# Windowed attention and two feed-forward layers on one core: weight tiles of two row halves, a 16-bit sign operation, and a new program order

## The chip, the cores and the metric

The kernel runs on one core of a Trainium2 chip. A core has TensorE (PE, the matrix engine; its weight loads are listed apart as PEld), VectorE (DVE), ScalarE (ACT), GpSimd (POOL) and SyncE (SP), which here only issues DMAs. The metric is the device time of one execution in microseconds, the median of the runs.

## The reference, cut to what matters

Attention with a window of 32 positions to each side plus 32 global positions, then a layer that takes the maximum of three products, then a gated layer. Batch 4, 8 heads, 512 local and 32 global positions, head size 64; 2,176 tokens of 512 features go through the two layers.

```python
s_ll = np.where(mask, scale * q_l @ k_l.T, -1e9)            # |i - j| <= 32
a_l = softmax(concat([scale * q_l @ k_g.T, s_ll]))
out_l = a_l @ concat([v_g, v_l])
out_g = softmax(scale * q_g @ concat([k_g, k_l]).T) @ concat([v_g, v_l])
x = concat([out_g, out_l])                                  # 2176 x 512
h = np.maximum(np.maximum(x @ w1, x @ w2), x @ w3)          # 512 -> 768
x = h @ w_out                                               # 768 -> 512
gate = 1.0 / (1.0 + np.exp(-(x @ w_gate)))                  # 512 -> 1536
out = (gate * (x @ w_val)) @ moe2_w_out                     # 1536 -> 512
```

The weights of both layers come as 64-bit floats, the rest as 32-bit floats.

## The kernel before

Attention is done in 32 units: a batch, a half of its positions, and a pair of heads. Four units make a chunk of 256 tokens (288 with the global ones, in every second chunk), so there are eight chunks. Of a unit, PE transposes queries and keys (units 0 to 7, line 532; later ones are transposed by DVE), makes the scores (619), global scores for pairs of units (645, 647), transposes the probabilities (683; later ones go through a DMA transpose) and makes the value products (770, later 780 and 785). In between DVE adds the mask and finds the maxima (625), ACT takes exponentials (661), DVE divides (675). The global rows of a batch have transposes (738) and value products (813, 849) of their own.

The first layer (`moe1_l1`) makes, for a chunk, a block of 128 of the 768 columns (six blocks, `f`) and each of the three matrices (`wi`), one product over four blocks of 128 rows; ACT or DVE folds it into the maximum (890, 893, 896). Chunk 0 uses the weights as plain 32-bit floats (882). The other chunks use a high part and a low part of weights and tokens, three matmuls for one (`mm3`, lines 321 to 323). The second layer (`moe1_l2`, line 918 for chunk 0) follows chunk by chunk. The gated layer (1038) and its output (1225) come last, as seven products for eight by a Strassen scheme.

Each weight tile of the first two layers is fetched and converted by `conv_a(i)`: 18 tiles of w1, w2 and w3 (`i = 3 f + wi`) and 6 of w_out, each 128 partitions by 512 pairs of words. A tile of w1 holds 128 columns and all four row blocks. `to_f32` turns a 64-bit float into a 32-bit one: ACT cuts the low word to three bits (285) and scales the high word (289), DVE puts the sign into the low word (291) and joins the two (294). Then ACT rounds the high part (312) and POOL subtracts it for the low part (271). The same `to_f32` serves the gated layer's weights (`w_prep`, 12 tiles of 1,024 elements) and its output weights (`wo_pre`, 6 of 1,024).

Every step of every unit, product and tile is an entry of a list; `ORDER`, a table of 3,388 numbers, says in which order the entries are issued, and by that the order of instructions on every engine and of the DMAs on SP's queue. An engine takes its instructions in that order, whatever they wait for.

Of the kernel before, what the change touches and what calls it, by code (L numbers as in the profile page):

```python
# [12 lines left out]
U32 = mybir.dt.uint32  # L13
AF = mybir.ActivationFunctionType
ALU = mybir.AluOpType
AX = mybir.AxisListType

P = 128
# [185 lines left out]
def kernel(  # L204
# [17 lines left out]
    nc = tc.nc  # L222
# [58 lines left out]
    def to_f32(raw, low_on_act, out=None):  # L281
# [4 lines left out]
        else:  # L286
            nc.vector.tensor_scalar(out=lo, in0=lo.bitcast(U32), scalar1=2.0 ** -29, scalar2=7.0, op0=ALU.mult, op1=ALU.min)
        yield
        nc.scalar.mul(f32(hi), f32(hi), 2.0 ** -112)
        yield  # L290
        nc.vector.scalar_tensor_tensor(out=lo, in0=hi, scalar=-2147483648, in1=lo,
                                       op0=ALU.bitwise_and, op1=ALU.bitwise_or)
        yield
        nc.vector.scalar_tensor_tensor(out=hi if out is None else out, in0=hi, scalar=3, in1=lo,
# [462 lines left out]
    xt = {}  # L757
# [719 lines left out]
```

## Time and profile before

| | |
|---|---|
| median of three runs | 809.6 us (809.15, 809.6, 814.51) |
| the profiled execution | 812.87 us, span 811.0 us |
| mean granted clock of PE | 0.996 |
| PE busy | 788.9 us, 97% |
| DVE busy | 599.6 us, 74% |
| ACT busy | 472.7 us, 58% |
| POOL busy | 148.8 us, 18% |

The span runs from the first to the last instruction; the time has 1.87 us more around it. A busy PE counts matmuls in flight, which overlap; where they come without a gap, PE sets the time of that stretch.

### The profile page before, as it was taken

The page shows a single profiled execution, that of the slowest core. Times are in us where ns is not written, and L with a number is a line of the kernel's source. Part 1 is how long each engine was busy: PE and PEld are TensorE (multiplying, and loading weights), DVE is VectorE, ACT ScalarE, POOL GpSimd, SP SyncE. Part 2 cuts the span into 40 slices and gives each one's busy share as a digit, 9 for nine tenths or more (in the row PEclk, how much of TensorE's full clock was granted, in tenths as well). Part 3 has the DMA queues.
Part 4 walks back from the last instruction along what each step waited for, and adds up shares of the span by engine and source line. Part 5 has one row for each costly group of instructions (what it writes and reads, how often), then busy time and mean ns, then how long its engine had stood idle before and what let it go on. Part 6 is the DMA issues. An engine that isn't in the chain of part 4 may idle for free.

```text
span 811.0 us, 18055 instructions
## 1 busy us (share of the span) xinstructions
PE 788.9 (97%) x6854; PEld 751.8 (93%) x6854; DVE 599.6 (74%) x1291; ACT 472.7 (58%) x1131; POOL 148.8 (18%) x149
## 2 busy tenths in 40 slices
PE   5999998999999999999999999999999999999998
PEld 3687798998999999899999999999999999999998
DVE  4799895876767676874876888788675858967773
ACT  6897775756446664563647656665636366444442
POOL 3241565243332413332120000000000000000000
PEclk9899999999999999999999999999999999999999
DMA  8998254545556553453425355956422469555411
GB/s 202 265 248 212 60 101 87 102 93 104 107 101 109 96 113 66 101 117 75 181 90 191 101 158 175 317 175 231 147 101 91 163 207 311 166 162 164 142 34 58
DMA packets 217590, 116.07 MB, mean 143 GB/s; under 512 B 161056, under 2 KB 204576, under 8 KB 217504
## 3 DMA queue, kind: packets, MB, share of 16 engines
q1 hardware_dynamic: 216960, 114.80, 52.2%
q8 instruction: 53, 0.87, 0.5%
q14 instruction: 33, 0.27, 0.1%
q10 hardware_dynamic: 544, 0.13, 0.1%
HBM read 74.91 MB, written 28.57 MB: 128 GB/s over the span
## 4 chain that ended last, share of the span: by engine, by line
PE 73%; SPq 8%; issue 6%; DMA 5%; DVE 3%; POOL 2%; ACT 2%; DVEq 0%; POOLq 0%; ACTq 0%
PE pa L1038 18%; PE pe L1038 9%; PE pa L1225 9%; PE ps L321 7%; PE ps L323 7%; PE ps L322 6%; PE pb L1038 4%; PE pe L1225 4%; PE pb L1225 2%; SPq L514 2%; SPq L513 2%; PE sp L619 2%; DMA vr<-in_v_g_dram 1%; PE ps L918 1%; POOL m L271 1%
## 5 line engine op out<-in xcount | busy, mean ns | idle before, releaser
L1038 PE MATMUL pa<-m,m 128*128 128x384 f32 (+1 forms) x864 | 154.1, 327 | 0.0
L321 PE MATMUL ps<-xt,m 128*128 128x288 f32 (+1 forms) x504 | 147.4, 292 | 3.5 <-DVE h L896 2.2
L323 PE MATMUL ps<-xt,m 128*128 128x288 f32 (+1 forms) x504 | 146.6, 291 | 0.0
L322 PE MATMUL ps<-xt,m 128*128 128x288 f32 (+1 forms) x504 | 145.3, 288 | 1.1 <-DVE xt L798 0.9
L1038 PEld LDWEIGHTS pa<-m,m 128*128 128x128 f32 x864 | 144.3, 188 | 0.2
L321 PEld LDWEIGHTS ps<-xt,m 128*128 128x128 f32 x504 | 94.8, 188 | 7.8 <-issue 2.7
L322 PEld LDWEIGHTS ps<-xt,m 128*128 128x128 f32 x504 | 94.7, 188 | 1.5 <-DVE xt L798 1.1
L323 PEld LDWEIGHTS ps<-xt,m 128*128 128x128 f32 x504 | 94.7, 188 | 0.0
L1044 ACT COPY sn<-pa 128x384 f32<-128x384 f32 (+1 forms) x108 | 49.0, 462 | 73.0 <-PE pa L1038 72.6
L1038 PE MATMUL pe<-m,m 128*128 128x384 f32 (+1 forms) x432 | 80.2, 327 | 0.0
L1038 PEld LDWEIGHTS pe<-m,m 128*128 128x128 f32 x432 | 72.5, 188 | 0.1
L1225 PE MATMUL pa<-m,m 128*128 128x256 f32 x576 | 71.9, 283 | 0.0
L1225 PEld LDWEIGHTS pa<-m,m 128*128 128x128 f32 x576 | 70.4, 192 | 0.1
L661 ACT ACTIVATE sm<-sm,st 128x224 f32<-128x224 f32 x128 | 60.8, 481 | 13.3 <-DVE st L625 13.0
L896 DVE TENSOR_TENSOR h<-ps,h 128x288 f32<-128x288 f32 (+1 forms) x90 | 38.9, 436 | 34.9 <-PE ps L323 23.5
L271 POOL TENSOR_TENSOR h<-h,h 128x288 fp32r<-128x288 f32 (+1 forms) x42 | 39.4, 942 | 103.1 <-ACT h L901 102.6
L707 DVE TENSOR_TENSOR pc<-sm,pc 64x512 f16<-64x512 f32 (+1 forms) x72 | 52.0, 723 | 8.1 <-ACT pc L704 6.9
L625 DVE CUSTOM_DVE_ANT_0 sm<-sp,mask 128x224 f32<-128x224 f32 x128 | 44.9, 381 | 7.9 <-PE sp L619 7.4
L321 PE MATMUL ps<-h,m 128*128 128x288 f32 (+1 forms) x168 | 49.4, 294 | 0.0
L1163 ACT CAST m<-m 128x768 fp32r<-128x768 f32 x44 | 35.8, 835 | 23.0 <-DVE m L1174 7.5
L704 ACT CAST pc<-sm 64x512 f16<-64x512 f32 (+1 forms) x72 | 39.3, 545 | 16.7 <-DVE sm L675 15.1
L323 PE MATMUL ps<-h,m 128*128 128x288 f32 (+1 forms) x168 | 48.9, 291 | 0.0
(193 smaller groups left out, 1628.7 us busy)
## 6 DMA issues: line engine op xcount, KB each, us to landing
m<-in_moe_w_dram SPq DMA_DIRECT2D x18, 512.0 KB, 5.5
gd<-sgt SPq DMA_DIRECT2D x48, 192.0 KB, 2.8
m<-gd SPq DMA_DIRECT2D x6, 1536.0 KB, 7.3
m<-in_moe_w_val_dram SPq DMA_DIRECT2D x6, 1024.0 KB, 5.3
wr<-in_moe_w_out_dram SPq DMA_DIRECT2D x6, 1024.0 KB, 6.0
m<-in_moe_w_gate_dram SPq DMA_DIRECT2D x5, 1024.0 KB, 7.6
vr<-in_v_l_dram SPq DMA_DIRECT2D x48, 96.0 KB, 2.5
x2d<-x2s SPq DMA_DIRECT2D x32, 128.0 KB, 2.0
```

Of the source, the lines that this page charges most:

```text
L271: nc.gpsimd.tensor_tensor(out=out, in0=a, in1=f32(b), op=ALU.subtract)
L321: nc.tensor.matmul(ps, lhsT=wh, rhs=xh, start=first, stop=False)
L322: nc.tensor.matmul(ps, lhsT=wh, rhs=xl, start=False, stop=False)
L323: nc.tensor.matmul(ps, lhsT=wl, rhs=xh, start=False, stop=last)
L625: nc.vector.tensor_tensor_reduce(out=sm[:, hh, j], in0=sp[hh][:, j, 0:224], in1=mask[:, half + j, :], scale=-SC, scalar=3.0e38, op0=ALU.ad ...
L661: nc.scalar.activation(sm4[:, i], sm4[:, i], AF.Exp, bias=st[:, 0, i:i + 1], scale=-1.0, accum_out=st[:, 2, i:i + 1])
L704: nc.scalar.copy(d, s_)
L707: nc.vector.tensor_tensor(out=l_, in0=s_, in1=h_, op=ALU.subtract)
L896: nc.vector.tensor_tensor(out=a, in0=ps[:, 0:n], in1=a, op=ALU.max)
L1038: nc.tensor.matmul(ps, lhsT=w[l][:, a, i], rhs=x[m][:, i], start=(k in (1, 2, 5) and i + l + m == 0), stop=(k in (2, 3, 4) and i == 1 and ...
L1044: nc.scalar.copy(t[:, 0:n], pend[u]["a"][:, 0:n])
L1225: nc.tensor.matmul(ps, lhsT=g[l][:, f], rhs=wo_op(b, f, m), start=(k in (1, 2, 5) and f + l + m == 0), stop=(k in (2, 3, 4) and f == 5 and ...
```

## The change

Three things. A tile of w1, w2 or w3 now holds 256 columns and two of the four row blocks (tile `f` of a pair `fp`: row half `kh`), so a product reads two tiles, and the runs in memory are twice as long. The sign word is made by an operation with one input: it takes the top 16 bits of the high word, keeps bit 15, and writes the top 16 bits of the low word, which are zero otherwise. And `ORDER` is another permutation of the same 3,388 entries.

```diff
+U16 = mybir.dt.uint16
...
 ORDER = [
-    153, 154, 57, 87, 0, 256, 56, 62, 63, 64, 67, 68, 69, 74, 58, 70, 71, 59, 1854, 161, 162, 95, 96, 75, 76, 77, 78,
...
-        nc.vector.scalar_tensor_tensor(out=lo, in0=hi, scalar=-2147483648, in1=lo,
-                                       op0=ALU.bitwise_and, op1=ALU.bitwise_or)
+        half = raw.bitcast(U16)
+        nc.vector.tensor_scalar(out=half[:, :, 1], in0=half[:, :, 3], scalar1=0x8000, scalar2=None, op0=ALU.bitwise_and)
...
     def conv_a(i):
         f, wi = divmod(i, 3) if i < 3 * NF1 else (i - 3 * NF1, 3)
+        fp, kh = divmod(f, 2)
...
-            nc.sync.dma_start(out=raw.rearrange("p (k f) t -> p k (f t)", k=KD),
-                              in_=src[:, f * 2 * P:(f + 1) * 2 * P].rearrange("(k p) f -> p k f", p=P))
+            nc.sync.dma_start(out=raw.rearrange("p (k f) t -> p k (f t)", k=2),
+                              in_=src[kh * 2 * P:(kh + 1) * 2 * P, fp * 4 * P:(fp + 1) * 4 * P].rearrange("(k p) f -> p k f", p=P))
...
     def moe1_l1(c, f, wi, hold):
+        cols = slice(P * (f % 2), P * (f % 2) + P)
+        tiles = [(wi, f - f % 2 + k // 2) for k in range(KD)]
...
-                nc.tensor.matmul(ps[:, 0:n], lhsT=ww[wi, f][:, k], rhs=xt[c, k][:, 0, 0:n], start=(k == 0), stop=(k == KD - 1))
+                nc.tensor.matmul(ps[:, 0:n], lhsT=ww[tiles[k]][:, k % 2, cols], rhs=xt[c, k][:, 0, 0:n], start=(k == 0), stop=(k == KD - 1))
...
-            wt = wa[wi, f]
+            wt = wa[tiles[k]]
...
-            mm3(ps[:, 0:n], (wt[:, 0, k], wt[:, 1, k]), (x[:, 0, 0:n], x[:, 1, 0:n]), k == 0, k == KD - 1)
+            mm3(ps[:, 0:n], (wt[:, 0, k % 2, cols], wt[:, 1, k % 2, cols]), (x[:, 0, 0:n], x[:, 1, 0:n]), k == 0, k == KD - 1)
```

Three places show the new order. In its rows the line numbers after the change are two to four higher; `tq` and `tk` are transposes of queries and keys, `sp` scores, `sg` global scores, `tp` transposes of probabilities, `ot` value products, `ps` with `xw` products of the first layer, and `m` with a number is a tile that was loaded (the numbers differ between the two kernels).

PE, the transposes of the second chunk's first unit (`m_289` before, `m_236` after) and what stands around them; before:

```order
L683 MATMUL tp<-ident,sm 128x128 x8
L619 MATMUL sp<-kw,qw 128x224 x4
L532 MATMUL tq<-ident,m_88 128x128 x2
L532 MATMUL tk<-ident,m_137 128x128 x2
L532 MATMUL tk<-ident,m_138 128x64
L532 MATMUL tq<-ident,m_289 128x128 x2
L532 MATMUL tk<-ident,m_258 128x128 x2
L532 MATMUL tk<-ident,m_259 128x64
L645 MATMUL sg<-kw,qgz_82 64x256 x2
L647 MATMUL sg<-kw,qgz_82 64x32 x2
```

and after:

```order
L685 MATMUL tp<-ident,sm 128x128 x8
L621 MATMUL sp<-kw,qw 128x224 x4
L647 MATMUL sg<-kw,qgz_82 64x256 x2
L649 MATMUL sg<-kw,qgz_82 64x32 x2
L534 MATMUL tq<-ident,m_236 128x128 x2
L534 MATMUL tk<-ident,m_287 128x128 x2
L534 MATMUL tk<-ident,m_288 128x64
```

The global scores of the first pair moved ahead of these transposes; those of the third unit, behind the scores before, stand further up.

PE, chunk 0 in the first layer, from the sixth unit's transposes on; before:

```order
L683 MATMUL tp<-ident,sm 128x128 x8
L619 MATMUL sp<-kw,qw 128x224 x4
L882 MATMUL ps_722<-xw,m_457 128x256 x4
L882 MATMUL ps_729<-xw,m_399 128x256 x4
L770 MATMUL ot<-pw,m_488 64x128 x16
L882 MATMUL ps_794<-xw,m_395 128x256 x4
L882 MATMUL ps_799<-xw,m_397 128x256 x4
L882 MATMUL ps_813<-xw,m_502 128x256 x4
L882 MATMUL ps_832<-xw,m_344 128x256 x4
L738 MATMUL tpg<-ident,eg 128x128 x5
L882 MATMUL ps_854<-xw,m_380 128x256 x4
L683 MATMUL tp<-ident,sm 128x128 x4
```

and after, from the score block on:

```order
L621 MATMUL sp<-kw,qw 128x224 x4
L772 MATMUL ot<-pw,m_581 64x128 x8
L886 MATMUL ps_741<-xw,m_577 128x256 x2
L886 MATMUL ps_741<-xw,m_544 128x256 x2
L886 MATMUL ps_755<-xw,m_529 128x256 x2
L886 MATMUL ps_755<-xw,m_594 128x256 x2
L886 MATMUL ps_761<-xw,m_529 128x256 x2
L886 MATMUL ps_761<-xw,m_594 128x256 x2
L740 MATMUL tpg<-ident,eg 128x128 x5
L886 MATMUL ps_780<-xw,m_639 128x256 x2
L886 MATMUL ps_780<-xw,m_574 128x256 x2
L772 MATMUL ot<-pw,m_581 64x128 x8
```

Each product has two tiles now; one unit's value products moved ahead of the first of this group, and the global transposes moved up.

DVE, the conversions behind the first six tiles; before, up to the tile of that group's second product (`m_399`):

```order
L291 SCALAR_TENSOR_TENSOR m_399<-m_399 128x512
L294 SCALAR_TENSOR_TENSOR m_395<-m_395 128x512
L294 SCALAR_TENSOR_TENSOR m_399<-m_399 128x512
L688 COPY pw<-tp 128x512
L625 ISA sm,st<-sp,mask 128x224
```

and after, up to the second tile of that group's first product (`m_544`):

```order
L293 TENSOR_SCALAR m_574<-m_574 128x512
L293 TENSOR_SCALAR m_577<-m_577 128x512
L295 SCALAR_TENSOR_TENSOR m_574<-m_574 128x512
L295 SCALAR_TENSOR_TENSOR m_577<-m_577 128x512
L293 TENSOR_SCALAR m_594<-m_594 128x512
L733 RECIPROCAL stg<-stg 128x1
L295 SCALAR_TENSOR_TENSOR m_594<-m_594 128x512
L293 TENSOR_SCALAR m_544<-m_544 128x512
L295 SCALAR_TENSOR_TENSOR m_544<-m_544 128x512
```

The tile that the second product of the group needed was the tenth to be joined; the first product of the new group needs the eleventh.

## Rows read from the trace of the kernel before

**Rows 1.** The page's first part: busy us (share of the span) and instructions.

```profile
PE 788.9 (97%) x6854; PEld 751.8 (93%) x6854; DVE 599.6 (74%) x1291; ACT 472.7 (58%) x1131; POOL 148.8 (18%) x149
```

**Rows 2.** Stages: length, busy PE, PEld, DVE, ACT, POOL, PE clock, DMA share, GB/s.

```profile
0.00:20.00 20.00, 11.66 (x53) 7.51 (x53) 9.51 (x37) 12.43 (x42) 6.39 (x26) 1.00 0.85 203
20.00:40.00 20.00, 17.98 (x149) 13.45 (x148) 15.33 (x39) 16.36 (x52) 4.39 (x3) 0.83 0.93 265
40.00:60.00 20.00, 19.77 (x130) 16.10 (x130) 19.02 (x47) 19.28 (x51) 8.87 (x6) 1.00 0.95 246
60.00:100.00 40.00, 37.56 (x243) 31.57 (x242) 37.54 (x90) 30.65 (x81) 14.26 (x11) 1.00 0.56 139
100.00:400.00 300.00, 294.23 (x3515) 277.42 (x3514) 212.18 (x604) 174.33 (x517) 107.93 (x98) 1.00 0.51 101
400.00:811.00 411.00, 407.68 (x2772) 405.77 (x2771) 306.07 (x478) 219.64 (x393) 6.94 (x6) 1.00 0.49 160
```

**Rows 3.** PE's waits: for whom, us in total, times, longest.

```profile
PE tq L532 <- DMA m<-in_q_l_dram: 8.1, 4, 3.6
PE ps L321 <- DVE h L896: 2.2, 1, 2.2
...
PE og L849 <- DMA ptg<-pcg: 1.2, 1, 1.2
...
PE ps L322 <- DVE xt L798: 0.9, 1, 0.9
...
PE ot L770 <- DVE pw L688: 0.7, 1, 0.7
```

**Rows 4.** PE's timeline, 19 to 24 us: start, length, instructions, idle time before.

```profile
19.73 0.30 PE L532 MATMUL tq<-ident,m 128*128 128x128 f32 x1 [3.61 <-DMA m<-in_q_l_dram]
20.95 0.48 PE L532 MATMUL tq<-ident,m 128*128 128x128 f32 x1 [0.92 <-DMA m<-in_q_l_dram]
...
22.08 1.12 PE L645 MATMUL sg<-kw,qgz 128*64 128x256 f32 x4
22.98 0.37 PE L647 MATMUL sg<-kw,qgz 128*64 128x32 f32 x4
```

**Rows 5.** Columns of rows 2, from 20.5 to 27.2 us.

```profile
20.50:27.20 6.70, 6.25 (x29) 4.42 (x30) 4.04 (x9) 3.75 (x13) 1.29 (x1) 0.50 0.86 252
```

**Rows 6.** DMA issues by line: count, KB each, median us to landing.

```profile
m<-in_moe_w_dram SPq DMA_DIRECT2D x18, 512.0 KB, 5.5
...
m<-in_moe_w_out_dram SPq DMA_DIRECT2D x6, 512.0 KB, 4.7
```

**Rows 7.** DVE's groups by form: count, busy us, mean ns of one, idle before.

```profile
L291 DVE SCALAR_TENSOR_TENSOR m<-m 128x512 int32<-128x512 int32 x24 | 19.5, 819 | 1.7 <-ACT m L289 1.6
...
L595 DVE CAST vb<-vr 128x512 bf16<-128x512 f32 x24 | 10.5, 440 | 16.4 <-POOL vr L593 13.1 <-DMA qr<-in_q_l_dram 3.1
...
L733 DVE TENSOR_SCALAR eg<-eg,stg 128x640 f32<-128x640 f32 x8 | 5.9, 734 | 0.2
```

**Rows 8.** DVE's timeline, three places between 53 and 91 us.

```profile
53.21 1.29 DVE L294 SCALAR_TENSOR_TENSOR m<-m 128x512 int32<-128x512 int32 x2
...
56.35 1.68 DVE L294 SCALAR_TENSOR_TENSOR m<-m 128x512 int32<-128x512 int32 x1
...
89.94 0.69 DVE L294 SCALAR_TENSOR_TENSOR m<-m 128x512 int32<-128x512 int32 x1
```

**Rows 9.** POOL's timeline from 54 us.

```profile
54.38 3.10 POOL L271 TENSOR_TENSOR m<-m,m 128x512 fp32r<-128x512 f32 x2 [6.96 <-ACT m L312]
```

**Rows 10.** PE's timeline, four places between 53 and 92 us.

```profile
53.23 3.73 PE L882 MATMUL ps<-xw,m 128*128 128x256 f32 x16
56.89 1.98 PE L770 MATMUL ot<-pw,m 96*64 96x128 f32 x32
...
69.58 0.66 PE L683 MATMUL tp<-ident,sm 128*128 128x128 f32 x4 [1.16 <-DVE pwg L744]
...
90.73 1.54 PE L918 MATMUL ps<-hw,m 128*128 128x256 f32 x6 [1.28 <-ACT vb L591]
```

More of the change, by code (lines that the diff above doesn't have):

```diff
@@ L308, in conv_a @@
         hi = f32(raw[:, :, 1])
-        ww[wi, f] = hi.rearrange("p (k f) -> p k f", k=KD) if cols else hi
+        ww[wi, f] = hi.rearrange("p (k f) -> p k f", k=2) if cols else hi
         yield
@@ L314, in conv_a @@
         sub(t[:, 1], hi, t[:, 0])
-        wa[wi, f] = t.rearrange("p l (k f) -> p l k f", k=KD) if cols else t
+        wa[wi, f] = t.rearrange("p l (k f) -> p l k f", k=2) if cols else t
         yield
```

337 rows, old and new, of the table ORDER are left out of this document.

## The prediction

> **What bounds the kernel now.** I read the engines' totals first, then the table by stage, then who makes TensorE (PE) wait, then the timeline at those places. PE is busy for 788.9 us of the 811.0 us span [rows 1], so all that any edit can return is the 22 us in which it is not, and what it does slowly. By stage [rows 2] PE lacks 8.3 us in the first 20 us, 2.0 in the next 20, 0.2 from 40 to 60, 2.4 from 60 to 100, 5.8 in the 300 us from 100 to 400, and 3.3 after 400, nearly all of which is the tail behind the last matmul. The last stage holds everything that the gated layer does; no reordering there can win. The reader is to see two more things in the same table. From 40 to 100 us VectorE (DVE) works 56.6 of 60 us and ScalarE (ACT) 49.9, so while PE looks full, DVE is as full, and it is DVE that hands PE its weights. And from 20 to 40 us the granted clock is 0.83: it is 0.50, the lower level of 1.2 GHz, from 20.5 to 27.2 us [rows 5], right after PE stood idle for 3.6 and 0.9 us.
>
> The waits of PE are few: 8.1 us in all for query rows, 3.6 of it in one piece, then single ones of 2.2, 1.2, 0.9 and 0.7 us [rows 3] and two of 1.2 and 1.3 in the stretch where DVE is full [rows 10]. The long one is in rows 4: the transposes of the second chunk's first unit begin at 19.73 us, when their query rows have landed, after 3.61 us of idle time; the second half begins at 20.95, and everything behind them on PE waits.
>
> **The change, part by part.** The sum is made against the profiled execution, 812.87 us (span 811.0 plus 1.87 around it), which lies 3.3 us above the median of the three runs, 809.6; differences carry over.
>
> *Loads.* Eighteen weight loads stay 512 KB each, but their runs in memory go from 1 KB to 2 KB, and the packets are halved. The nearest row is the six loads of the output matrix, also 512 KB, whose runs are 4 KB: 4.7 us to landing against 5.5 [rows 6]. So each load gains between 0 and 0.8 us. The DMA engines are 0.85 to 0.95 busy for the first 60 us [rows 2], so shorter traffic is real there, but only where PE waits for a load. That is the one place of rows 4: three weight loads are queued on SP ahead of the second chunk's rows, before and after alike, and the bytes ahead are the same. Three times 0.8 would be 2.4, but they overlap in flight and PE waits for the rows behind them; I take 0.4 (from 0 to 2.4).
>
> *Sign word.* 42 operations with two inputs become operations with one. 18 of them (1,024 elements) lie behind 400 us, where PE waits for nothing: 0. The 24 of 512 elements took 0.819 us each [rows 7], 0.69 when alone, and an operation of the same kind beside a GpSimd subtraction took 1.68 [rows 8, 9]. The new form is not in the trace. Bounds: the one-input cast of 512 elements took 0.440 us, and the one-input operation with a scalar on 640 took 0.734 [rows 7], which scaled to 512 at its own 1.15 ns an element is 0.59. I take the middle, 0.52, since the instruction is that of the second row and the width nearer that of the first: 0.30 saved, 24 times, 7.2 us of DVE work (5.5 to 9.1), all of it between 12 and 93 us, where DVE is the fuller engine.
>
> The Trainium skill ("VectorE: DVE Perf Modes", section "Mode 2×_2P — use both read ports for one tensor") says that an operation with one source in SBUF handles two elements a cycle, fp32 included; by it I estimate 512 / 2 / 0.96 GHz plus the row's overhead, 0.34 us. The 734 ns row with one source [rows 7] does not agree, as it ran near one element a cycle. By the rule the saving would be 11.5 us of DVE work instead of 7.2, and the forecast below about 1 us lower. "SBUF — State Buffer", section "Who interferes with whom", speaks against that: in such a two-port mode the operation would go on colliding with GpSimd's, as the two-input one did at 56.35 us.
>
> *Tiles of two row halves.* A product of the first layer now reads two tiles of a pair of column blocks, not one tile with all four row blocks. The first six products need the same six tiles as before. The next group began at 53.23 us on PE [rows 10], and DVE had closed the tenth conversion at 54.50 [rows 8]. In the new order the group's first product needs the eleventh. One more conversion is 0.69 + 0.69 us, so 55.9 at the old pace; eleven cheaper sign words take 3.3 off: 52.6. PE arrives at 53.23 plus 0.99 (half of the 1.98 us of value products [rows 10], of which one unit's now stands ahead) less the 2.4 gained so far (below): 51.8. So a wait of 0.8, from 0 to 4.1; ACT, 19.3 of 20 us busy there [rows 2], may add to it, and I take 1.0.
>
> *Order on PE.* (1) The global-score matmuls of the first pair, at 22.08 to 23.35 at the low clock [rows 4], move ahead of the stuck transposes into idle time: 1.3. (2) The value product that waited 0.7 us for a copy of DVE [rows 3] gets a score block and a value block between its transposes and itself: 0.7. (3) The probability transposes that waited 1.2 us at 69.6 for the copy of the global transposes [rows 10]: between these two stood one product, 1.9 us (half of the 3.73 in rows 10); now it is three products, a value block and a score block, over 7 us: 1.2. (4) The second layer of chunk 0 stood for 1.28 us until 90.73 [rows 10]. The wait is put down to ACT, but DVE's last step on an output-matrix tile ran from 89.94 to 90.63 [rows 8], and this is what ends it. That tile, 23rd to be converted before, is 21st now; the one that is 23rd now is needed two matmuls later, and DVE is ahead by its savings: 1.3. (5) Past 100 us there are waits of 2.2, 1.2 and 0.9 us [rows 3] and shorter ones. A new order removes some and makes others; nothing in the order says which, so 0 (from -4.3 to +4.3). (6) The gated layer's first products move ahead of the last blocks of the second layer. PE has no gap around 400 us to fill: 0, covered by the preparation that runs on DVE and ACT, half idle there.
>
> Sum: -0.4 -1.3 -0.7 -1.2 -1.3 +1.0 = -3.9 us, hence 809.0 for the profiled execution and 809.6 - 3.9 = **805.7 us** for the median.
>
> **Rivals.** *The clock holds.* With the 1.3 us of scores in it the idle time shrinks from 3.6 to some 2 us. If the clock then stays at 2.4 GHz, the 6.25 us that PE works between 20.5 and 27.2 [rows 5] shrink by up to 3.1; DVE and ACT, 4.0 and 3.8 of 6.7 busy, would let 2.6 of it through: 803.1. Against it: the moved scores take 1.3 us at the low clock and half of that at the higher one, so 2 to 3 us stay in which PE has nothing ready.
>
> *A larger gain.* The clock holds and the three waits past 100 us go too: 803.1 - 4.3 = 798.8. For it speaks only that the waits are single and each has slack next to it.
>
> *Nothing in the end.* The sign word is no shorter than 0.69, or ACT, which loses no work, sets the pace from 40 to 60; then (4) fails and the pair wait costs 3 instead of 1: 805.7 + 1.3 + 2.0 = 809.0.
>
> *Slower.* The pair rule bites. The place is the seventh product of chunk 0 on PE; the mechanism is that two conversions must be done where one was enough, so PE stands for 4.1 us. This is longer than the 3.6 us after which the clock fell in rows 4 and 5, so 3.1 us more go at 1.2 GHz; the next two products wait for the twelfth conversion the same way, some 1.4 us each. With (1) to (3) still gained: 809.6 - 3.2 + 4.1 + 3.1 + 2.8 = 816.4. It decides from the point at which the eleventh conversion ends later than 54 us.
>
> **How the numbers follow.** The forecast (803.5 to 807.8) gets 0.42, nothing in the end 0.24, the clock 0.13, the larger gain 0.08, slower 0.13. Two in ten lie outside 798 to 815: a part of the larger gain, and the upper half of the slower case with what the order past 100 us could add to it. A change of under 1% (8.1 us) can hardly be told from none here, and what PE leaves open makes more than that unlikely on either side: below 801.5 us stand the larger gain, a quarter of the clock case and the low end of (5), 0.16; above 817.7 a half of the slower case, 0.07; within, 0.77.
>
> **What would show it.** Right: the row of the sign word near 0.5 us; no wait of over 0.3 us before the value product near 35 us, the transposes near 69 and the second layer near 89; the global scores ahead of the second chunk's transposes, with the gap still there but shorter. Wrong: a wait of several us on PE at the seventh product of chunk 0 (near 52 us); a clock below 0.83 in the first 100 us; PE's idle time from 100 to 400 us above 8 us; or any gap behind 400 us, where I have put the moved products at nothing.

## The result, and the profile after

The changed kernel took 816.95 us (median of 6 runs, 815.32 to 818.28) against 810.15 for the kernel before (6 runs): a ratio of 1.0079, 95% interval 1.0057 to 1.0102. A second measurement gave 814.74 against 808.99: 1.0068, 1.0042 to 1.0093. The change makes the kernel slower by some 6 us, where 805.7 and a gain of 3.9 had been forecast. 816.95 lies above the range of 798 to 815.

The profiled execution took 818.28 us, span 816.5. The page's first part (busy us, share of the span, instructions), to be read beside [rows 1]:

```profile
PE 794.5 (97%) x6854; PEld 755.1 (92%) x6854; DVE 601.7 (74%) x1291; ACT 471.4 (58%) x1131; POOL 146.5 (18%) x149
```

PE is idle for 816.5 - 794.5 = 22.0 us, as before (22.1). It spends 5.6 us more being busy on the same 6,854 matmuls. So the first question is not who makes PE wait longer in total, but where it works more slowly, and the table by stage (columns as in [rows 2]; the last two rows are stretches of their own) answers a part of it:

```profile
0.00:20.00 20.00, 12.92 (x62) 8.28 (x62) 9.52 (x36) 12.87 (x44) 6.36 (x26) 1.00 0.94 219
20.00:40.00 20.00, 17.58 (x134) 14.04 (x135) 16.06 (x47) 15.85 (x53) 0.00 (x0) 0.74 1.02 274
40.00:60.00 20.00, 19.48 (x120) 15.87 (x119) 19.41 (x42) 18.15 (x48) 9.45 (x7) 1.00 0.64 167
60.00:100.00 40.00, 37.89 (x260) 31.03 (x259) 37.05 (x81) 30.24 (x79) 17.53 (x13) 1.00 0.66 168
100.00:400.00 300.00, 294.31 (x3485) 276.83 (x3484) 206.40 (x606) 171.03 (x513) 107.72 (x98) 0.99 0.51 101
21.50:31.70 10.20, 8.67 (x45) 6.92 (x45) 6.37 (x18) 6.79 (x24) 0.00 (x0) 0.50 1.00 275
171.80:175.20 3.40, 3.20 (x15) 3.20 (x16) 1.14 (x3) 2.22 (x10) 0.00 (x0) 0.51 0.43 67
```

The granted clock is at its lower level, 1.2 GHz, for 10.2 us in the early part (6.7 before, [rows 5]) and for another 3.4 us from 171.8. PE is busy for 8.7 + 3.2 = 11.9 us at that level, against 6.3 before; half of the difference, 2.8 us, is work that the full clock would not have taken.

To place the rest, count every matmul of both traces at the mean spacing of its kind, and compare when each kernel has done the same amount of this work. The changed kernel begins 1.2 us later. It stands 1.1 us behind near 100 us and 0.4 near 165. Then it loses 3.9 us between 165 and 180, stands 3.6 behind at 400, and 5.5 at the end: 1.1 by 100 us, 2.5 from 100 to 400, 1.9 after 400. These are two single executions, 2.7 and 1.3 us above the medians of their kernels, and that of the kernel before has a loss of its own, 2.6 us between 320 and 345, which the traces of two of the runs below with the same order up to there (the sign word alone, the last stage alone) lack. Set against the trace of the sign word alone (809.69 us), the changed kernel's second trace (814.68 us) is 1.3 us behind at 100 us, 0.2 ahead at 283, 1.7 behind at 303, 2.2 at 398 and 5.0 at the end. The waits of PE (columns as in [rows 3]) name some of the places:

```profile
PE ps L323 <- ACT h L894: 3.2, 4, 2.4
PE tk L534 <- DVE qw L555: 2.9, 1, 2.9
...
PE ps L922 <- ACT xt L798: 1.3, 1, 1.3
...
PE pa L1042 <- ACT sgt L1064: 0.7, 1, 0.7
PE ps L886 <- DVE m L295: 0.5, 1, 0.5
```

**Near 17 us.** The global scores moved ahead of the second chunk's transposes, as the order said, and the query rows had landed by 17.5 us instead of 19.7 [rows 4]. The new order asks for them 7.4 us earlier, ahead of this chunk's key rows and no longer behind them; SP's row for these two loads, before and after:

```profile
16.25 1.08 SPq L432 DMA_DIRECT2D m<-in_q_l_dram  x2
8.89 1.17 SPq L434 DMA_DIRECT2D m<-in_q_l_dram  x2
```

PE's timeline shows what came instead:

```profile
16.82 0.65 PE L647 MATMUL sg<-kw,qgz 128*64 128x256 f32 x4
17.30 0.26 PE L649 MATMUL sg<-kw,qgz 128*64 128x32 f32 x4
17.49 0.44 PE L534 MATMUL tq<-ident,m 128*128 128x128 f32 x2
20.83 0.61 PE L534 MATMUL tk<-ident,m 128*128 128x128 f32 x3 [2.91 <-DVE qw L555]
```

The transposes of the keys wait 2.91 us for an accumulator that DVE's copy of an earlier unit's queries frees. DVE's timeline has that copy at 20.28, behind two conversions and a third sign word (mask steps between them are left out):

```profile
15.73 0.75 DVE L293 TENSOR_SCALAR m<-m 128x512 uint16<-128x512 uint16 x1
16.52 0.69 DVE L295 SCALAR_TENSOR_TENSOR m<-m 128x512 int32<-128x512 int32 x1
17.13 0.74 DVE L293 TENSOR_SCALAR m<-m 128x512 uint16<-128x512 uint16 x1
17.90 0.69 DVE L295 SCALAR_TENSOR_TENSOR m<-m 128x512 int32<-128x512 int32 x1
...
19.75 0.73 DVE L293 TENSOR_SCALAR m<-m 128x512 uint16<-128x512 uint16 x1
20.28 0.45 DVE L555 COPY qw<-tq 128x256 f32<-128x256 f32 x1
```

The gap has changed its cause, from a DMA to an engine that is full, and it is hardly shorter: 2.9 us for 3.6.

**The sign word.** DVE's groups by form (as [rows 7]):

```profile
L293 DVE TENSOR_SCALAR m<-m 128x512 uint16<-128x512 uint16 x24 | 18.6, 794 | 0.0
L293 DVE TENSOR_SCALAR m<-m 128x1024 uint16<-128x1024 uint16 x11 | 14.8, 1341 | 2.9 <-ACT m L290 2.9
L293 DVE TENSOR_SCALAR wr<-wr 128x1024 uint16<-128x1024 uint16 x7 | 9.5, 1361 | 3.2 <-ACT wr L290 3.2
```

0.794 us instead of 0.819 on average, where 0.52 had been taken. The means hold some longer ones (up to 1.9 us before, 1.2 after); by the medians it is 0.74 us instead of 0.69. And the 18 long ones are slower, 1.34 to 1.36 us for 1.22.

**Near 169 us.** The step of 3.9 us is one wait and the clock behind it. On ACT:

```profile
168.60 0.62 ACT L593 CAST vb<-vr 128x512 bf16<-128x512 f32 x1 [1.57 <-DMA vr<-in_v_g_dram]
169.25 1.05 ACT L706 CAST pc<-sm 64x512 f16<-64x512 f32 x2
170.20 0.40 ACT L905 CAST h<-h 128x256 fp32r<-128x256 f32 x1
171.58 0.37 ACT L894 COPY h<-ps 128x256 f32<-128x256 f32 x1 [0.98 <-POOL h L272]
```

On POOL, and on PE:

```profile
169.36 1.15 POOL L595 TENSOR_TENSOR vr<-vr,vb 128x512 f32<-128x512 f32 x1 [6.34 <-ACT vb L593]
170.68 0.87 POOL L272 TENSOR_TENSOR h<-h,h 128x256 fp32r<-128x256 f32 x1 [0.17 <-ACT h L905]
```

```profile
169.34 0.28 PE L325 MATMUL ps<-xt,m 128*128 128x256 f32 x1
172.00 0.58 PE L323 MATMUL ps<-xt,m 128*128 128x256 f32 x1 [2.38 <-ACT h L894]
```

Read from the end: PE needs an accumulator, which ACT's copy (L894) empties into a buffer that POOL (L272) must have read, which needs ACT's rounding (L905). That rounding stands on ACT behind the preparation of the values of unit 14 (L593), which waits 1.57 us for the last of four DMAs that the new order issues only just ahead of it, from 164.1 to 166.1 us. PE stands for 2.38 us, and goes on at the lower clock.

### The profile page after: what moved, and what is told of

It is laid out like the page before. It is cut to its first block, busy times and chain, and to the rows that moved or that the text cites. A ratio compares the mean times of both kernels' runs of the same rounds, so it can differ in the third digit from the quotient of the medians.

```text
span 816.5 us, 18058 instructions
## 1 busy us (share of the span) xinstructions
PE 794.5 (97%) x6854; PEld 755.1 (92%) x6854; DVE 601.7 (74%) x1291; ACT 471.4 (58%) x1131; POOL 146.5 (18%) x149
## 4 chain that ended last, share of the span: by engine, by line
PE 76%; DVE 9%; ACT 5%; SPq 4%; DMA 3%; issue 2%; POOL 1%; DVEq 0%; POOLq 0%; ACTq 0%
PE pa L1042 16%; PE pa L1229 8%; PE pe L1042 8%; PE ps L323 7%; PE ps L325 7%; PE ps L324 7%; PE pe L1229 4%; PE pb L1042 4%; PE sp L621 2%; PE ps L886 2%; PE pb L1229 2%; DVE pc L709 2%; PE ps L922 1%; PE ot L782 1%; PE acc L1206 1%
## 5 line engine op out<-in xcount | busy, mean ns | idle before, releaser
L1042 PE MATMUL pa<-m,m 128*128 128x384 f32 (+1 forms) x864 | 156.1, 327 | 0.7 <-ACT sgt L1064 0.7
L709 DVE TENSOR_TENSOR pc<-sm,pc 64x512 f16<-64x512 f32 (+1 forms) x72 | 50.0, 695 | 11.3 <-ACT pc L706 9.9
L1172 DVE TENSOR_TENSOR m<-m,m 128x768 fp32r<-128x768 f32 x44 | 41.0, 955 | 23.0 <-ACT m L1167 22.4
L272 POOL TENSOR_TENSOR h<-h,h 128x288 fp32r<-128x288 f32 (+1 forms) x42 | 35.6, 852 | 102.4 <-ACT h L905 97.2
L323 PE MATMUL ps<-h,m 128*128 128x288 f32 (+1 forms) x168 | 49.4, 294 | 1.0 <-DVE h L900 1.0
L325 PE MATMUL ps<-h,m 128*128 128x288 f32 (+1 forms) x168 | 48.8, 290 | 0.0
L324 PE MATMUL ps<-h,m 128*128 128x288 f32 (+1 forms) x168 | 48.4, 288 | 0.0
```

The costliest lines, as they stand in the source:

```text
L272: nc.gpsimd.tensor_tensor(out=out, in0=a, in1=f32(b), op=ALU.subtract)
L323: nc.tensor.matmul(ps, lhsT=wh, rhs=xh, start=first, stop=False)
L324: nc.tensor.matmul(ps, lhsT=wh, rhs=xl, start=False, stop=False)
L325: nc.tensor.matmul(ps, lhsT=wl, rhs=xh, start=False, stop=last)
L709: nc.vector.tensor_tensor(out=l_, in0=s_, in1=h_, op=ALU.subtract)
L1042: nc.tensor.matmul(ps, lhsT=w[l][:, a, i], rhs=x[m][:, i], start=(k in (1, 2, 5) and i + l + m == 0), stop=(k in (2, 3, 4) and i == 1 and ...
```

## The experiments

Each run gives its median, and the ratio to runs of the kernel before on the same chip with its 95% interval. That kernel's own runs spread over 806 to 813 us, so intervals are some 4 us wide; where less matters, the traces are compared by the same matmul work. Theory O was that the new order costs the time; S blamed the sign word, T the tiles.

**The parts one by one.** The first adds the sign word's lines of the diff to the kernel before; the second gives the kernel before the new table; the third takes the sign word's lines out of the changed kernel:

```diff
 # first                                  # second                 # third
-nc.vector.scalar_tensor_tensor(...)     -ORDER = [153, 154, ...   -nc.vector.tensor_scalar(out=half...)
+nc.vector.tensor_scalar(out=half...)    +ORDER = [56, 57, ...     +nc.vector.scalar_tensor_tensor(...)
```

The sign word alone: 

> The kernel before with the new sign operation alone (old tiles, old order). Theory O (the new order costs the time: a later first DMA, and a wait of 2.4 us near 169 us that is followed by the low clock): 809 to 811, no change, because the 24 operations of 512 elements took 0.794 us after and 0.819 before, and PE waits for nothing behind 400 us. Theory S (the sign operation costs it, since its form of 1,024 elements took 1.341 us after and 1.221 before and its short form gained nothing): 814 to 817.

The order alone: 

> The kernel before with the new order alone (old tiles, old sign operation). Theory O: 815 to 818, with the wait near 169 us and the low clock behind it in the trace. Theory S: 809 to 811. Theory T (the pairs of tiles cost it): 809 to 811.

The changed kernel with the old sign word: 

> The changed kernel with the old sign operation (new tiles, new order). Theory O: 815 to 817, and nothing to tell it from the run with the order alone. Theory S: 809 to 811. Theory T: 815 to 817, but 5 above the run with the order alone.

Measured: the sign word alone 810.01, 1.0017 (0.9996 to 1.0037), nothing to tell from no change. The order alone 817.12, **1.0109** (1.0079 to 1.0139), some 8.8 us slower. Order and tiles without the new sign word 814.30, 1.0071 (1.0045 to 1.0097), the same as the whole change (1.0068 and 1.0079). S and T fall: it is the order, and the tiles, far from costing, give back some 3 us of it. PE's waits from 36 to 60 us in the run with the order alone show where some of it lies:

```profile
PE ps L883 <- DVE m L295: 2.9, 2, 1.6
```

Twice PE waits for the join of a tile, 2.9 us in all. In the third run, which differs from this one by the tiles alone, that row reads 0.9, and in the changed kernel 0.5. The new order joins the tiles in the order that pairs need.

**The wait near 169.** Three entries of `ORDER`, the first steps of the values of unit 14, go behind ACT's copy (entry 1451):

```diff
-... 592, 1437, 612, 619, 620, 621, 583, 613, 614, 1452, 615, 1472, 1473, 353, 1361, 616, 1451, ...
+... 592, 1437, 612, 583, 613, 614, 1452, 615, 1472, 1473, 353, 1361, 616, 1451, 619, 620, 621, ...
```

> The changed kernel with three entries moved: the preparation of the value rows of unit 14, whose first step stands on ACT for a DMA issued 4.5 us before, comes behind the copy that frees the product's accumulator. Theory O: the wait of 2.4 us at 169 shrinks below 0.6 and the clock stays at 1.00 there, so 816.9 less 3.5, 813.4 (812.5 to 814.5). Rival M (the wait only moves, to the value products of unit 14 or to the next copy): 816 to 817, with another wait of over 1.5 us between 165 and 185 us.

And the changed kernel again: 

> The changed kernel again, to stand beside the runs of the same call: 816 to 818, 8 above the kernel before. Whether its low clock near 171 us comes again: theory O says that the wait of over 2 us at 169 stands in the trace again, and that the clock behind it may fall or not.

Measured: 813.32 (812.33 to 814.48) with the entries moved, 1.0060 (1.0037 to 1.0083); the changed kernel again 814.74 (813.83 to 815.24). In the trace with the move, PE works without a break there, at the full clock:

```profile
165.00:175.00 10.00, 10.00 (x170) 9.48 (x169) 7.75 (x17) 6.86 (x19) 4.46 (x4) 1.00 0.56 100
```

The changed kernel's second trace has the wait again, but 1.29 us long, and the clock holds:

```profile
169.52 0.39 PE L323 MATMUL ps<-xt,m 128*128 128x256 f32 x1 [1.29 <-ACT h L894]
...
169.50:171.00 1.50, 1.48 (x12) 1.48 (x13) 0.80 (x2) 1.50 (x7) 0.00 (x0) 1.00 0.44 69
```

So the wait belongs to the order, and costs 1.4 us in one execution and 3.9, with the clock, in another. Between the two medians lie 1.4 us, by the ratios 0.6; the two were timed on different chips and the intervals of the ratios overlap, so the price in time is not secured.

**The first DMA.** In `ORDER`, entry 57 (the first query rows) goes ahead of 56 (the first key rows):

```diff
-ORDER = [56, 57, 59, 0, 223, ...
+ORDER = [57, 56, 59, 0, 223, ...
```

> The changed kernel with one entry moved: the first query rows are asked for ahead of the first key rows, as in the kernel before. Theory Q (the late start of 1.2 us is passed on to the end): the first transposes begin near 3.1 us, and 1.2 less than the changed kernel. Rival A (it is absorbed by the later waits for copies and rows, up to 30 us): within 0.4 of the changed kernel.

Measured: 814.37, 1.0070 (1.0044 to 1.0097). The first transpose begins at 3.08 us again, and PE then meets the wait for DVE's copy 0.7 us earlier, 2.90 us long as before. Rival A: the late start is real and costs nothing that can be measured.

**The last stage alone.** The kernel before, with the order of its last 1,478 entries (from the first product of the last chunk on) taken from the changed kernel:

```diff
+tail = ORDER_after[1910:]
+ORDER = [n for n in ORDER_before if n not in tail] + tail
```

> The kernel before, its order unchanged up to the seventh chunk, and the new order from the first product of the last chunk on (some 410 us to the end). Theory G (the new order of the gated layer costs 1.9 us by itself): 1.5 to 2.3 above the kernel before, with the waits of 0.8 and 0.5 us near 450 and 515 us. Rival H (those waits come from what stands ahead of them, in the chunks): within 0.5 of the kernel before.

Measured: 810.90, 1.0023 (1.0003 to 1.0042), 1.9 us slower, and its trace loses 2.0 us behind 390 us. PE's waits behind 400 us, where the kernel before has none, are

```profile
PE pa L1039 <- ACT sgt L1061: 0.6, 1, 0.6
PE pe L1039 <- DVE tm L1058: 0.4, 1, 0.4
```

Theory G holds: ACT does a weight conversion (1.1 us) ahead of the sigmoid whose input PE must overwrite. These two waits make up 1.0 us of it; the rest was not placed. Counted by matmul work against the trace of the sign word alone, the other traces with the whole new order and either of the kernels' own sign words lose 1.3 to 2.8 us behind 400, and those with the old order there nothing.

**The tiles in the old order.** The same kernel with the new tiles. Six tiles change places in the conversions, so that the first products find their pairs, and their buffers go with them; three conversions of high parts come later:

```diff
+_PERM = {1: 2, 2: 1, 11: 6, 6: 11, 14: 16, 16: 14}   # tile numbers in ORDER and in SLOT
```

> The run before this one with the new tiles: the tiles of a pair take the places of the old order, six of them exchanged so that both tiles of a product are ready, and three conversions of high parts come later. Theory P (the tiles gain by shorter loads, as they did in the new order, by 2.8 us): 2 to 3.5 below the run with the new tail alone. Rival W (in an order that wasn't made for pairs PE waits for the second tile): 0 to 4 above it, with waits for DVE's join of over 1 us between 38 and 80 us.

Measured: 827.61, 1.0228 (1.0203 to 1.0253), 16.7 us above the run without the tiles. Its waits:

```profile
PE ps L889 <- DVE m L298: 9.8, 4, 4.9
PE tq L537 <- DMA m<-in_q_l_dram: 5.6, 5, 3.1
```

9.8 us of waits for joins, and a clock of 0.51 from 82 to 89 us, which falls near the end of the wait of 4.9 us (78.6 to 83.5). That is the mechanism of the prediction's slower rival, two joins needed where one was enough, in the old order. Rival W names it as well, but had put it at 0 to 4 us; what the three later conversions add to the 16.7 was not taken apart.

**DVE's copy near 17 us.** Entry 129 goes ahead of two conversions:

```diff
-... 175, 176, 1857, 1858, 1829, 1830, ... 1864, 109, 129, 1833, ...
+... 175, 176, 129, 1857, 1858, 1829, 1830, ... 1864, 109, 1833, ...
```

> The changed kernel with one entry moved: DVE's copy of the third unit's transposed queries, which frees the accumulator that PE's transposes wait for at 17.5 us, comes ahead of two conversions (2.8 us of DVE work) instead of behind them. Theory E (that wait is the price of the early part): the wait of 2.9 us shrinks below 1, the low clock is shorter than the 10.2 us seen in the runs with the new order, and 1 to 2.5 less than the changed kernel (ratio to before 1.004 to 1.006). Rival F (DVE and ACT are full from 40 to 60 us, so what PE gains by 20 us is waited for again by 60): the wait shrinks all the same, but the time is within 0.5 of the changed kernel (ratio 1.006 to 1.008).

Measured: 815.10, 1.0084 (1.0063 to 1.0105), no gain. PE's timeline:

```profile
17.90 0.27 PE L535 MATMUL tk<-ident,m 128*128 128x128 f32 x1
18.85 0.33 PE L535 MATMUL tk<-ident,m 128*128 128x128 f32 x1 [0.68 <-DMA m<-in_k_l_dram]
19.77 0.24 PE L535 MATMUL tk<-ident,m 64*128 64x64 f32 x1 [0.58 <-DMA m<-in_k_g_dram]
22.40 0.90 PE L622 MATMUL sp<-kw,qw 64*128 64x224 f32 x4 [2.38 <-ACT kw L560]
```

The wait for DVE is gone, and in its place stand 0.68 and 0.58 us for key rows and 2.38 for ACT. Rival F: rows, DVE and ACT are all late at 20 us, and a wait taken from one is found at the next. The low clock lasts 3.4 us instead of 10.2 as well, and the time is no shorter for it.

**What the sign word would have given.** The same operation on 32-bit words. It overwrites the low word, so the three lowest bits of each weight are left out:

```diff
-        nc.vector.scalar_tensor_tensor(out=lo, in0=hi, scalar=-2147483648, in1=lo,
-                                       op0=ALU.bitwise_and, op1=ALU.bitwise_or)
+        nc.vector.tensor_scalar(out=lo, in0=hi, scalar1=-2147483648, scalar2=None, op0=ALU.bitwise_and)
```

In the kernel before, a single run: 

> The kernel before with the sign word made by an operation with one input of 32 bits, which overwrites the low word; it leaves out the three low bits that the low word gives to the result. Only the operation's time is looked at. Theory I (one input is what makes it shorter, and the 16-bit steps took that back): 0.44 to 0.60 us for 512 elements. Rival J (the pace is set by the elements with gaps between them, whatever the inputs): 0.67 to 0.72 when alone, 1.2 for 1,024 elements.

The same, timed: 

> The kernel before with the sign word by an operation with one input of 32 bits, timed (the three low bits of the result are left out). Theory I (what a shorter sign operation gives in the old order): 803 to 805, a ratio to before of 0.994 to 0.996; the waits near 88, 138, 321 and 342 us are shorter or gone, since DVE is ahead. Rival K (the single look was a low one of a spread of 6 us): 806 to 808, a ratio of 0.998 to 1.

In the changed kernel: 

> The changed kernel with that same operation of 32 bits in place of the one of 16 bits (the three low bits are left out). Theory R (the prediction failed at two places that add: the price of the sign operation and the new order's own waits): 3 to 5 below the changed kernel, 809 to 812, a ratio to before of 1.001 to 1.004, still slower. Rival N (the order is made for a short sign operation and only loses with a long one): 804 to 806, a ratio below 0.998, with the waits near 17, 55 and 168 us gone.

In the kernel before, and without ACT's step on the low word: 

> The first kernel of this call without ACT's step on the low word, which nothing reads any more there (42 ACT steps of 0.67 to 1.14 us less; the three low bits are left out as before). Theory L (ACT, 19.3 of 20 us busy from 40 to 60, is the next limit there once DVE is shorter): 1 to 3 below the first kernel, 801 to 803. Rival B (the early waits are for rows and DVE, so ACT's time is free): within 0.7 of it.

DVE's groups in the single run:

```profile
L291 DVE TENSOR_SCALAR m<-m 128x512 int32<-128x512 int32 x24 | 14.6, 614 | 1.5 <-ACT m L289 1.3
L291 DVE TENSOR_SCALAR m<-m 128x1024 int32<-128x1024 int32 x11 | 7.6, 691 | 5.3 <-ACT m L289 5.3
```

Theory I, with its price a little off: 0.614 us for 512 elements on average, 0.38 to 0.43 for the 16 that began while GpSimd was idle, 0.691 for 1,024. With one input the operation on 32-bit words takes 0.42 us where it took 0.69 with two; 16-bit elements at the same step of 8 bytes took that back. The Trainium skill ("VectorE: DVE Perf Modes", section "Mode 2×_2P — use both read ports for one tensor") gives two elements a cycle to an operation with one source in SBUF. These rows agree: from 0.42 to 0.691 us a further element costs 0.53 ns, half of the 1.04 ns of the operation with two inputs (0.69 to 1.22 us). The row of 640 elements in [rows 7], which the prediction set against that rule, is a mean that hides two kinds of rows (ns min/median/max, first and last start, in the kernel before):

```profile
L733 DVE TENSOR_SCALAR eg<-eg,stg x8: 543/554/1419, 62.8 to 366.6; 128x640 f32<-128x640 f32 x8
```

Six of the eight took 0.54 to 0.55 us, near the 0.49 that these rows give for 640 elements (an estimate); the two others, 1.16 and 1.42 us, began while a subtraction of GpSimd ran.

In time: 807.26 in the old order, 0.9985 (0.9962 to 1.0007), some 1.2 us less, which the interval does not secure (the single run, 804.14, was low in its spread), as rival K has it. In the changed kernel 810.68, **1.0020** (1.0004 to 1.0036): 4 us below the changed kernel, and still not faster than before. Theory R. Its trace has the same waits, 2.6 us for DVE's copy at 17, 2.3 for ACT at 20, 1.6 near 166. Without ACT's step 807.68, 0.9980 (0.9962 to 0.9997), as with it: rival B, ACT's time is free there.

**All moves together.** The changed kernel with the entries of three runs above moved, and two ACT steps of weight conversion put behind the sigmoid that PE waits for (seven entries in all):

```diff
+move 57 before 56; 129 before 1857; 619, 620, 621 behind 1451
+move 3016 (L290) behind 2419 (L1064); 3145 (L286) behind 2517 (L1064)
```

> The changed kernel with eight entries moved: the one of the run before the last, the first query rows ahead of the first key rows, the value rows of unit 14 later, and in the gated layer two ACT steps of weight conversion behind the sigmoid that PE waits for (those near 447 and 496 us). Theory O (the named waits are what the order costs): no wait of PE over 0.5 us near 168, 447 and 496 us, and 3 to 5 less than the changed kernel, which is about 1 to 3 above the kernel before (ratio 1.001 to 1.004). Rival M (other waits take their places): less than 2 below the changed kernel (ratio over 1.005).

Measured: 813.18 (811.98 to 813.71), 1.0061 (1.0041 to 1.0082). The waits over 0.5 us near 168, 447 and 496 us are gone from the trace, and its span is 2.7 us shorter than that of the changed kernel's second trace; the median is 1.6 us lower, by the ratios 0.6, on another chip. That is rival M by its numbers: the named waits are a part of the order's cost, and not the larger one. No version with the full bits beat the kernel before.

## Why the prediction was wrong

What failed is "Order on PE", in two steps. The first is the sum itself: it counts (1) to (4), 4.5 us, as gained because four waits of the old trace go. Where the sum has 3.9 us gained by 100 us, the changed kernel is 1.1 us behind there (1.3 in its second trace against the sign word alone): a wait of 2.9 us for DVE's copy and others stand in their place. The second is (5) and (6), "nothing in the order says which, so 0", and for the gated layer "0, covered by the preparation that runs on DVE and ACT, half idle there". By the same two comparisons the changed kernel loses 2.5 or 0.9 us from 100 to 400 us, and 1.9 or 2.8 behind. With the old tiles and the old sign word the new order costs 8.8 us. The prediction listed the waits that the new order removes, which the trace of before shows, and priced at zero those that it makes, which that trace cannot show. A third miss, the price of the sign word, adds to both. Two of the prediction's own signs of being wrong came: a clock of 0.74 from 20 to 40 us, and gaps behind 400. Point by point:

- **Loads** (-0.4): 4.6 us to landing for 5.5 [rows 6], but two other traces with the old tiles and the old order up to there (the sign word alone, the last stage alone) have 5.1. In the new order the tiles make it 4.6 for 4.9 (third run against second), in the old order 5.4: the longer runs in memory give some 0.3 us or nothing. The second chunk's query rows were there 2.2 us earlier, by the order and not by the tiles: "the bytes ahead are the same" was a misreading, since the key rows had moved behind them. PE had no use for it, since DVE's copy was the next wait: nothing gained.
- **Sign word** (0.52 us, 7.2 us of DVE work saved): 0.794 measured, 0.6 us of DVE work saved in the first 100 us and 2.3 lost behind 400. The bounds were two one-input operations that read 32-bit words side by side; neither was near a 16-bit access in steps of 8 bytes. The upper bound was misread besides: its 734 ns are a mean of six rows of 0.55 us and two of 1.2 and 1.4, so the trace of before did not speak against the rule that the prediction set aside, and the single rows would have made the forecast lower still. Had the price been right, the change would still have been 0.2% slower (the run with 32-bit words in the changed kernel): of the 10 us between forecast and result, some 4 to 5 hang on this price. Part of that lies behind 400 us, where the prediction had 0: the trace of that run loses 0.8 us there, the changed kernel's second 2.8.
- **Pairs** (+1.0): 0.5 us by the row for DVE's join, at 56.10 us, where the seventh product needs its second tile. The place and the cause are right, the size by luck: the eleventh join ended at 55.96 us (52.6 forecast) and PE came to this product at 54.45 (51.8), both some 3 us late. That the tiles are worth some 3 us in the new order and cost 16.7 in the old was not foreseen, as they were priced inside one order.
- **(1)** (-1.3): the scores moved, and the next thing, DVE's copy, was late by 2.9 us. Right about the place, wrong about what is next. The low clock became longer (10.2 us for 6.7), not shorter.
- **(2), (3)** (-0.7, -1.2): both waits are gone from the trace. By 100 us nothing of it is left: the changed kernel is 1.1 us behind. DVE, ACT and the rows are all near their limit up to 60 us, which the prediction had read in [rows 2] and used only for the pairs; that this is what took the gain back is shown near 20 us alone, by the run with DVE's copy moved.
- **(4)** (-1.3): the wait is still there, 1.32 us at 90.68, behind DVE's 21st join, which ends at 90.58. The prediction had it gone because the sign word would put DVE ahead; with the 32-bit word in the changed kernel it is 0.86 us, so the price of the sign word is about a third of it.
- **(5)** (0, bounds ±4.3): +2.5 between the two profiled executions, 0.9 between the two nearer their medians, so inside the bounds. The wait near 169 is a new one. Its load stands three entries ahead of its reader on ACT; but it stands only five ahead in the kernel before, where ACT waits 0.42 us for it and PE does not. New is that the rounding on which POOL, the copy and PE hang stands behind that reader. The trace of before shows that such loads come late for ACT, though not what the new order would put behind them:

```profile
ACT vb L591 <- DMA vr<-in_v_g_dram: 20.4, 11, 4.0
```

A larger loss has no single name: by matmul work against the sign word alone, all nine traces with the new order fall back by 1.9 us or more (up to 3.5, in the run with the order alone) between 283 and 303 us, those with the old order by 0.6 at most. PE's waits for DVE there are of 0.2 to 0.8 us, and no run moved anything there.
- **(6)** (0): +1.9 (0.2 to 3.4 by the interval), shown by the run with the new tail alone. DVE and ACT are half idle there on average, but ACT's order matters at single places.

None of the rivals was it. *Slower* had another mechanism; its condition, an eleventh conversion that ends later than 54 us, came true at 55.96 without its wait of 4.1 us, since PE was late as well. And *Nothing in the end* had the sign word right and stopped at no gain.

What stays open: the moves of the last experiment take away 0.6 to 1.6 of the 6 us in time (2.7 between two traces). Against the sign word alone, the trace with these moves still loses 1.0 us by 100 us, 2.2 between 283 and 303 and 1.3 behind 400; none of these was taken apart. Why the low clock lasts 10.2 us in five of the traces with the new order and 3.4 to 6.8 in four others was not settled either; the times of single runs show little of it.

## What to carry to other kernels

Price a new order on both sides: for each load that moves, compare the distance to its first reader on the in-order engine with the time from issue to landing, and ask what else stands behind that reader. Where DVE, ACT and the DMAs are all full, a wait taken from one is found at the next; only the trace of the changed kernel shows which. And take a price for a new operation only from rows with its element size and its step in memory, not from its number of inputs alone, and from single rows, not from a mean that mixes in those beside GpSimd.

## What the runs showed of the hardware

- A one-input bitwise operation that reads and writes 16-bit elements 8 bytes apart is slower per element than the two-input one on 32-bit words: from 704 ns (the fastest of 512) to 1,332 (the fastest of 1,024) that is 1.23 ns an element, against 1.04 (0.69 to 1.22 us) with two inputs and 0.53 (0.42 to 0.69 us) with one input of 32 bits, 8 bytes apart as well. The first and the last from the views of these lines in the changed kernel and in the single run (columns: ns min/median/max, first and last start):

```profile
L293 DVE TENSOR_SCALAR m<-m x35: 704/767/1354, 15.7 to 626.8; 128x512 uint16<-128x512 uint16 x24, 128x1024 uint16<-128x1024 uint16 x11
```

```profile
L291 DVE TENSOR_SCALAR m<-m x35: 378/682/1634, 15.0 to 617.7; 128x512 int32<-128x512 int32 x24, 128x1024 int32<-128x1024 int32 x11
```

- The fast form waits for GpSimd. In the single run with 32-bit words, 16 of the 24 operations of 512 elements began while GpSimd was idle and took 0.38 to 0.43 us. The other eight began while a GpSimd instruction ran and took 0.52 to 1.63 us; each ended 0.28 to 0.29 us behind the end of that instruction (the longest one, from 80.80, behind the next, which followed at once). In the kernel before, six two-input ones ended 0.55 us behind it in the same way. One of the eight, and what it met:

```profile
56.47 1.13 DVE L291 TENSOR_SCALAR m<-m 128x512 int32<-128x512 int32 x1
56.00 1.31 POOL L271 TENSOR_TENSOR m<-m,m 128x512 fp32r<-128x512 f32 x1 [1.29 <-ACT m L311]
```

- The granted clock fell at the end of a wait of 2.38 us near 170 and held behind one of 1.29 at the same place. In the run with the order alone it fell at 300.3 us, 2.3 us behind a wait of only 0.75, and stayed low for 3.3 us in which PE was busy without a break:

```profile
300.25:303.50 3.25, 3.25 (x51) 2.35 (x47) 1.98 (x7) 2.00 (x7) 0.00 (x0) 0.51 0.42 91
```
